# Attention decode over a long cache: the softmax of a four-head chunk taken in two halves, and the last chunks' transfers cut differently

## The chip, the cores and the metric

The kernel runs on one core of a Trainium2 chip. A core has a matrix engine (PE, whose weight loads are listed as PEld), a vector engine (DVE), a scalar engine (ACT), a general engine (POOL), a sequencer that issues transfers (SP), and 16 DMA engines that bring data from HBM to SBUF. Matmuls write to PSUM. The metric is the device time of the whole kernel in microseconds (us). Of the kernel before, four executions were timed: 1372.18, 1374.35, 1375.49 and 1377.13 us, median 1374.92.

## The reference

There are two attention layers with one query per batch row (4 rows, model width 512, 32 heads of 128) over cached keys and values. The first, A, looks at a window of 2048 keys with eight key/value heads; the second, B, at all 8192 keys with 32 heads of its own. The outputs stand side by side.

```python
def _B_ref(x, k_cache, v_cache, wq, wo):        # k_cache, v_cache: [4, 32, 8192, 128] bf16
    q = (x @ wq).reshape(B, Sq, H, Dh).transpose(0, 2, 1, 3)
    scores = jnp.einsum("bhqd,bhkd->bhqk", q, k_cache) * (Dh ** -0.5)
    p = _softmax(scores, axis=-1)
    o = jnp.einsum("bhqk,bhkd->bhqd", p, v_cache)
    return o.transpose(0, 2, 1, 3).reshape(B, Sq, H * Dh) @ wo
```

B's caches are 2 x 268 MB, so nearly all of the 587 MB that the kernel reads is theirs, and each byte is used once.

## The kernel before, in words

The work is cut into 40 chunks. Chunks 0 to 7 are A's (one key/value head each, all batch rows). Chunks 8 to 39 are B's: one batch row and four heads each, with 8.4 MB of keys and 8.4 MB of values. The four heads lie on the partitions, 32 partitions to a head, and each partition holds 64 KB of keys: 256 tiles (`NTB`) of 128 x 128. Tiles go in groups of eight (`TG`), 32 groups to a chunk. `NC` is 40, `NCA` is 8.

One chunk of B (`whole_B`) runs as follows.

1. Keys. For each group, PE transposes eight tiles into a PSUM bank (`emit_T`, bank `tr`), DVE (two of three groups) or ACT (the third) copies them to SBUF (`kt`), and PE multiplies them with the query (`emit_S`, two groups behind, `SLAG`), which leaves the scores in `sc`, one PSUM bank for each half of the keys.
2. Softmax. DVE takes the row maximum of each half (`stats_rowmax`), the first among the scores, and combines the two. PE transposes the maxima (`stats_gmax`), DVE reduces them per head, PE spreads them back over the partitions (`stats_bc`), DVE scales them to `negb`, and ACT takes twelve exps (`exp_B`: three parts of the keys, four heads each) into `pbb`.
3. While this goes on, PE multiplies the rows of B's output weights into another order (`reorder`, four heads; DVE copies each to `wol` with `take_wol`) and runs a few matmuls whose result nobody reads (`keep_busy`).
4. PV. PE multiplies 256 value tiles with the exps, all into one sum in `po` (`emit_pv`). `norm_sum` sums the row sums over the partitions and inverts them, `norm_out` scales `po`. The multiplication with the output weights (`emit_fin`) stands at the second group of the next chunk.

Each engine executes its own list in order, and the lists are written out by the order of the calls in `whole_B`. The wait for an event holds back everything behind it on that engine. The loop over B's chunks is a loop on PE, DVE and ACT; SP and POOL have straight lists.

Transfers are all in SP's list, in the order keys, (for every fourth chunk the output weights `wos`), values (`dma_K`, `dma_V`). Keys land in units 0 to 3 of the buffer `kv`, values in units 4 to 7. The second half of each is then copied by POOL into units 8 and 9 (`KX`), which keys and values share, so a unit is free once its half has been copied. A transfer of keys is issued once the first quarters of the keys before it have been transposed and their second half copied. A transfer of values waits until the first half of the PV before it is done (`("pv", c, 2)`) and the second half of those values has been copied; the copies of values into `KX` wait for the transposes of the keys that lie there. `wos` waits for the fourth `reorder` of the chunk before.

A transfer can be cut into pieces, each with its own semaphore, so that work can begin on a part: `HALVES`, `NEXTK` (four quarters), `NEXTV` (128, 64, 32 and 32 tiles), `LASTK`, `LASTV`. Before the change, keys came in halves in chunks 30 to 34 and in quarters in chunks 35 to 38; values came in halves in chunk 36 and in `NEXTV` in chunks 37 and 38. The last chunk's are cut finest. All other transfers are whole.

The lines of the profile that matter: L475 (transposes) and L477 (all other matmuls), L541 and L543 (copies of transposed keys on ACT and DVE), L612 and L615 (row maximum), L641 (`negb`), L661 (exps), L666 (row sums), L778 (`wol`), L752 (`norm_out`), L372 (POOL's copies), L392 (issue of keys), L355 (of `wos`), L429 (of values).

## Time and profile before

| what | value |
|---|---|
| timed runs, median | 1374.92 us |
| the profiled execution, its own time | 1371.9 us |
| its span, first to last instruction | 1370.1 us |
| PE busy | 1239.1 us (90%) |
| PEld busy | 1114.0 us (81%) |
| DVE busy | 766.9 us (56%) |
| ACT busy | 547.3 us (40%) |
| POOL busy | 469.8 us (34%) |
| HBM read | 587.21 MB, 429 GB/s over the span |
| granted clock of PE, mean | 0.968 |

The span goes from the first to the last instruction on the core; the execution's own time is 1.8 us longer. Busy shares are means over the whole span, and the stages of a chunk use the engines quite differently: PE is nearly always busy among the scores, ACT only copies there, and the exps come in one block behind them. PE's matmuls are pipelined and their ends are modelled, so that a busy PE is not necessarily at its peak. The groups of instructions with the most time:

| line, engine, operation | count | busy us | mean ns |
|---|---|---|---|
| L475 PE, transposes of keys | 8704 | 671.0 | 222 |
| L543 DVE, copies of transposed keys | 736 | 502.1 | 691 |
| L372 POOL, copies of second halves | 248 | 459.9 | 1896 |
| L477 PE, scores of B | 8192 | 399.8 (first form listed) | 192 |
| L541 ACT, copies of transposed keys | 352 | 359.6 | 1024 |
| L477 PE, PV of B | 8192 | 263.2 | 196 |
| L661 ACT, exps of B | 384 | 171.1 | 446 |
| L612 DVE, row maximum of a half | 64 | 43.9 | 686 |
| L666 DVE, row sums | 32 | 39.0 | 1220 |

The durations of single matmuls overlap: the mean of one is longer than the distance from one to the next.

### The profile page before, as it was taken

What the parts mean: (1) busy time and instruction counts of PE and PEld (TensorE: products, weight loads), DVE (VectorE), ACT (ScalarE), POOL (GpSimd) and SP (SyncE); (2) the same over time, 40 slices, a digit from 0 to 9 for tenths busy, and PEclk for the clock granted to TensorE, in tenths of its full rate; (3) what the DMA queues carried; (4) which work ended last, traced back from release to release, by engine and by line L of the source; (5) the groups of instructions that cost most, each with busy time, mean ns of one, the idle gap of its engine ahead of it and who ended that gap; (6) DMA issues with size and microseconds to landing.
All of it is one profiled execution on the core that took longest, in us unless ns stands there. A gap on an engine that the chain in (4) does not pass through costs nothing.

```text
span 1370.1 us, 61779 instructions
## 1 busy us (share of the span) xinstructions
PE 1239.1 (90%) x27640; PEld 1114.0 (81%) x27673; DVE 766.9 (56%) x1335; ACT 547.3 (40%) x777; POOL 469.8 (34%) x277
## 2 busy tenths in 40 slices
PE   4897799988999989888999899998999999999998
PEld 4776688887888878877888788887888888888887
DVE  1775465554555655555556555554565665645555
ACT  1553343443434434433444333433444443433443
POOL 2000244334433443344334433443344334443342
PEclk9998899999999999999999999999999999999999
DMA  9999999999999999999999999999999999999998
GB/s 399 425 427 440 431 427 436 427 438 430 430 436 419 444 438 432 429 430 442 429 429 430 442 429 429 438 435 429 434 430 430 433 433 440 429 422 429 426 426 350
DMA packets 19359, 587.54 MB, mean 429 GB/s; under 512 B 2164, under 2 KB 2184, under 8 KB 4616
## 3 DMA queue, kind: packets, MB, share of 16 engines
q1 hardware_dynamic: 19304, 587.21, 99.6%
q8 instruction: 15, 0.25, 0.1%
q14 instruction: 8, 0.07, 0.0%
q10 hardware_dynamic: 32, 0.01, 0.0%
HBM read 587.21 MB, written 0.01 MB: 429 GB/s over the span
## 4 chain that ended last, share of the span: by engine, by line
DMA 56%; PE 37%; DVE 2%; issue 2%; POOL 2%; ACT 0%; SPq 0%; POOLq 0%; DVEq 0%
DMA kv<-in_B_k_cache_dram 40%; PE tr L475 20%; DMA kv<-in_B_v_cache_dram 11%; PE sc L477 9%; PE po L477 5%; DMA kv<-in_A_k_cache_dram 2%; DMA kv<-in_B_wq_dram 2%; POOL kv L372 2%; PE fin L477 2%; PE ms L477 1%; PE tr L477 1%; DVE rm L615 0%; DVE kt L543 0%; DVE sA L596 0%; DVE wor L778 0%
## 5 line engine op out<-in xcount | busy, mean ns | idle before, releaser
L372 POOL COPY kv<-kv 128x2048 int32<-128x2048 int32 x248 | 459.9, 1896 | 877.3 <-DMA kv<-in_B_k_cache_dram 288.2
L475 PE MATMUL tr<-identb,kv 128*128 128x128 bf16 x8704 | 671.0, 222 | 52.0 <-POOLq L75 44.0
L543 DVE COPY kt<-tr 128x1024 bf16<-128x1024 bf16 x736 | 502.1, 691 | 267.1 <-PE tr L475 264.6
L541 ACT ACTIVATE kt<-tr 128x1024 bf16<-128x1024 bf16 x352 | 359.6, 1024 | 662.6 <-PE tr L475 662.4
L475 PEld LDWEIGHTS tr<-identb,kv 128*128 128x128 bf16 x8704 | 512.6, 99 | 66.0 <-issue 46.7
L477 PE MATMUL sc<-qq,kt 128*128 128x64 bf16 x8192 | 399.8, 192 | 12.5 <-DVE kt L543 9.8
L477 PEld LDWEIGHTS sc<-qq,kt 128*128 128x128 bf16 x8192 | 333.3, 98 | 16.2 <-DVE kt L543 13.1
L477 PEld LDWEIGHTS po<-pbb,kv 128*128 128x128 bf16 x8192 | 260.5, 100 | 22.1 <-issue 10.2
L477 PE MATMUL po<-pbb,kv 128*128 128x64 bf16 x8192 | 263.2, 196 | 10.8 <-POOL kv L372 4.9
L661 ACT ACTIVATE pbb<-sc,negb 32x64 bf16<-32x64 f32 (+1 forms) x384 | 171.1, 446 | 143.7 <-DVE negb L641 138.5
L666 DVE TENSOR_REDUCE rsb<-pbb 128x4 f32<-128x1024 bf16 x32 | 39.0, 1220 | 97.9 <-ACT pbb L661 97.9
L778 DVE CAST wor<-tr 128x512 bf16<-128x512 f32 x128 | 80.3, 684 | 2.9 <-PE tr L477 2.9
L477 PE MATMUL tr<-wos,back 32*128 32x512 bf16 x512 | 69.6, 383 | 3.1
L477 PE MATMUL po<-sel,identb 128*128 128x512 bf16 x224 | 68.5, 401 | 0.0
L477 PEld LDWEIGHTS po<-sel,identb 128*128 128x128 bf16 x256 | 20.1, 99 | 39.5 <-issue 30.7
L612 DVE TENSOR_REDUCE rh<-sc 128x4 f32<-128x512 f32 x64 | 43.9, 686 | 14.3 <-PE sc L477 14.3
L477 PEld LDWEIGHTS tr<-wos,back 32*128 32x128 bf16 x512 | 21.7, 93 | 34.4 <-DVE wor L778 19.2
L752 DVE TENSOR_TENSOR oz<-po,rz 128x16 bf16<-128x16 f32 x32 | 5.6, 175 | 68.9 <-PE po L477 68.9
L730 DVE RECIPROCAL rinv<-ms 128x4 f32<-128x4 f32 (+1 forms) x40 | 7.8, 196 | 49.6 <-PE ms L477 49.6
L475 PE MATMUL ms<-identf,rm 128*4 128x128 f32 x40 | 10.9, 272 | 20.5 <-DVE rm L615 17.9
L477 PE MATMUL sc<-qb,kt 128*128 128x64 bf16 (+3 forms) x512 | 25.4, 194 | 0.8 <-DVE gx L633 0.6
L477 PE MATMUL po<-pba,kv 128*128 128x64 bf16 x512 | 20.5, 199 | 3.7 <-issue 2.4
(65 smaller groups left out, 284.4 us busy)
## 6 DMA issues: line engine op xcount, KB each, us to landing
kv<-in_B_k_cache_dram SPq DMA_DIRECT2D x12, 4096.0 KB, 26.4
kv<-in_B_k_cache_dram SPq DMA_DIRECT2D x17, 2048.0 KB, 30.1
kv<-in_B_v_cache_dram SPq DMA_DIRECT2D x5, 4096.0 KB, 28.9
kv<-in_A_k_cache_dram SPq DMA_DIRECT2D x8, 2048.0 KB, 14.5
kv<-in_A_v_cache_dram SPq DMA_DIRECT2D x8, 2048.0 KB, 16.0
kv<-in_B_v_cache_dram SPq DMA_DIRECT2D x3, 2048.0 KB, 27.3
kv<-in_B_k_cache_dram SPq DMA_DIRECT2D x6, 1024.0 KB, 31.5
kv<-in_B_v_cache_dram SPq DMA_DIRECT2D x5, 1024.0 KB, 31.4
```

The lines of the kernel that those rows point to most:

```text
L372: lambda e, x=x: e.tensor_copy(flat(KX, 2)[:, x].bitcast(I32), flat(units, 2)[:, x].bitcast(I32)),
L475: sch.add("pe", lambda e: e.transpose(o, l, r), waits, key)
L477: sch.add("pe", lambda e: e.matmul(o, l, r, start=start, stop=stop), waits, key)
L541: sch.add("act", lambda e: e.activation(dst, src, ACTF.Copy), waits=waits, key=("ev", s))
L543: sch.add("dve", lambda e: e.tensor_copy(dst, src), waits=waits, key=("ev", s))
L612: sch.add("dve", lambda e: e.tensor_reduce(out=rh[:, half, :], in_=src, axis=AX.X, op=ALU.max), waits=[("S", ch["s"] + (half + 1) * ch["NG ...
L661: sch.add("act", lambda e, src=src, dst=dst, pp=pp, u=u: e.activation(dst, src, ACTF.Exp, bias=negb[pp, 0, u:u + 1], scale=scale), waits=[ ...
L666: sch.add("dve", lambda e: e.tensor_reduce(out=rst[1][:, :], in_=probs_of(c).rearrange("p j u -> p u j"), axis=AX.X, op=ALU.add), waits=[( ...
L730: sch.add("dve", lambda e: e.reciprocal(out=ri, in_=ms[:, L0:L0 + n]), waits=[("L", c)], key=("rinv", c))
L752: sch.add("dve", lambda e: e.tensor_tensor(out=o, in0=i0, in1=i1, op=ALU.mult), waits=waits, key=("oT", c))
L778: sch.add("dve", lambda e: e.tensor_copy(wol[:, u, :], o), waits=[("reord", c) if u == 3 else ("reord", c, u)] + [("fin", prev(c))], key=( ...
```

## The change

Each half of the keys gets a maximum of its own. The first half's maximum, its spreading and its exps are placed among the scores of the second half, at fixed groups (`HEADS_AT`). PV of the first half stands right behind the last score; the second half's maximum and exps are placed between its groups. Between the halves, DVE multiplies the sum in `po` with exp of the difference of the two maxima (`fade_B`, `fade_out_B`), into `fd`, and a matmul with the identity brings it back into PSUM as the start of the second half's sum. The row sums are taken per half and joined in the same way. `keep_busy` is gone. The first three `reorder` stand between the halves, the fourth at group 22 of PV, behind `norm_sum`. The first transposes of the next chunk wait for `wol`.

The pieces change too: keys are cut in the last four chunks (halves in 36 and 37, quarters in 38, the last as before), and values in the last three (halves in 37, `NEXTV` in 38, the last as before).

```diff
-        PIECES_K.update({c: ("d_fk", HALVES) for c in range(NC - 10, NC - 5)})
-        PIECES_K.update({c: ("d_nk", NEXTK) for c in range(NC - 5, NC - 1)})
-        PIECES_V = {NC - 4: ("d_hv", HALVES), NC - 3: ("d_nv", NEXTV), NC - 2: ("d_nv", NEXTV), NC - 1: ("d_lv", LASTV)}
+        PIECES_K.update({NC - 4: ("d_fk", HALVES), NC - 3: ("d_fk", HALVES), NC - 2: ("d_nk", NEXTK)})
+        PIECES_V = {NC - 3: ("d_hv", HALVES), NC - 2: ("d_nv", NEXTV), NC - 1: ("d_lv", LASTV)}
...
+                    if c > NCA and g < NTRB:
+                        waits += [("wol", c - 1, 3 if g == 0 else g)]
...
+        HEADS_AT = {23: (0,), 26: (1,), 29: (2, 3)}
...
-        EXPS = ((0, NTB // 4), (NTB // 4, NTB // 2), (NTB // 2, NTB))
-
-        def exp_B(c):
...
+        def exp_B(c, half, heads):
+            for u in heads:
+                pp = HEADS[u][1]
+                src = sc[pp, half, :].rearrange("p (j u) -> p u j", u=4)[:, u, :]
+                dst = probs_B(half)[pp, :, u]
+                waits = [("negb", c, half), ("c_pb", 1)] + ([("pv", c - 1), ("rs", c - 1)] if c > NCA else []) if u == 0 else []
+                sch.add("act", lambda e, src=src, dst=dst, pp=pp, u=u: e.activation(dst, src, ACTF.Exp, bias=negb[pp, half, u:u + 1], scale=scale),
+                        waits=waits, key=("exp", c, half) if u == 3 else None)
...
+        def fade_B(c):
+            sch.add("dve", lambda e: e.tensor_tensor(out=hs[:, 2, :], in0=negb[:, 1, :], in1=negb[:, 0, :], op=ALU.subtract),
+                    waits=[("negb", c, 1)], key=("gap", c))
+            sch.add("act", lambda e: e.activation(hs[:, 3, :], hs[:, 2, :], ACTF.Exp),
+                    waits=[("gap", c)] + ([("rs", c - 1)] if c > NCA else []), key=("fade", c))
+
+        def part_sums_B(c, half):
+            sch.add("dve", lambda e: e.tensor_reduce(out=hs[:, half, :], in_=probs_B(half).rearrange("p j u -> p u j"), axis=AX.X, op=ALU.add),
+                    waits=[("exp", c, half)], key=("psum", c, half))
+
+        def fade_out_B(c):
+            sch.add("dve", lambda e: e.tensor_tensor(
+                out=fd[:, :].rearrange("p (x u) -> p x u", u=4), in0=po[:, 0:NW].rearrange("p (x u) -> p x u", u=4),
+                in1=bcast(hs[:, 3, :], [[0, NW // 4], [1, 4]]), op=ALU.mult),
+                waits=[("pv", c, 2), ("fade", c)], key=("faded", c))
+
         def sums_B(c):
-            sch.add("dve", lambda e: e.tensor_reduce(out=rst[1][:, :], in_=probs_of(c).rearrange("p j u -> p u j"), axis=AX.X, op=ALU.add),
-                    waits=[("exp", c, 2)] + rs_read[NSM], key=("rs", c))
+            sch.add("dve", lambda e: e.tensor_tensor(out=hs[:, 0, :], in0=hs[:, 0, :], in1=hs[:, 3, :], op=ALU.mult),
+                    waits=[("psum", c, 0), ("fade", c)], key=("fsum", c))
+            sch.add("dve", lambda e: e.tensor_tensor(out=rst[1][:, :], in0=hs[:, 0, :], in1=hs[:, 1, :], op=ALU.add),
+                    waits=[("fsum", c), ("psum", c, 1)] + rs_read[NSM], key=("rs", c))
...
-                for k in (1, 2):
-                    if c >= NCA and j == EXPS[k][0] - NW // 4:
-                        waits = [("exp", c, k)]
+                half = c >= NCA and j == NTB // 2
+                if half:
+                    waits = [("exp", c, 1)]
+                    pe_mm(po[:, base:base + n], identf[:, :], fd[:, :], stop=False, waits=[("faded", c)], key=("fdmm", c))
...
-        def keep_busy(n):
-
-            for _ in range(n):
-                pe_mm(po[:, :], identb[:, :], sel4[:, :, :].rearrange("p r x -> p (r x)"))
...
-                if g == ch["NG"] // 2 + SLAG + 1:
+                if g == 19:
                     stats_rowmax(c, 0)
+                if g == 21:
+                    stats_gmax(c, 0)
+                if g == 23:
+                    stats_bc(c, 0)
+                if g in HEADS_AT:
+                    exp_B(c, 0, HEADS_AT[g])
             for g in range(SLAG):
                 emit_S(ch["s_last"] + 1 - SLAG + g)
             stats_rowmax(c, 1)
-            reorder(c, 0, 0)
-            reorder(c, 1, 1)
-            reorder(c, 2, 2)
-            keep_busy(1)
-            stats_gmax(c)
-            keep_busy(1)
-            stats_bc(c)
-            exp_B(c)
-            for u in range(3):
-                take_wol(c, u, u)
-            keep_busy(3)
-            reorder(c, 3, 0)
-            keep_busy(3)
-            take_wol(c, 3, 0)
-            sums_B(c)
             for g in range(ch["NG"]):
                 emit_pv(c, g)
-                if g == 20:
+                if g == 3:
+                    stats_gmax(c, 1)
+                if g == 6:
+                    stats_bc(c, 1)
+                    fade_B(c)
+                    exp_B(c, 1, range(4))
+                    part_sums_B(c, 0)
+                if g == ch["NG"] // 2 - 1:
+                    for u in range(3):
+                        reorder(c, u, u)
+                    fade_out_B(c)
+                    part_sums_B(c, 1)
+                    sums_B(c)
+                    for u in range(3):
+                        take_wol(c, u, u)
+                if g == 22:
                     norm_sum(c)
+                    reorder(c, 3, 0)
+                    take_wol(c, 3, 0)
             norm_out(c)
```

## The prediction

> **What bounds the kernel now.** I read four views in this order: the page's slices, a table of windows, the timeline of one chunk, and the chain of waits. The slices and the queue table come first:
>
> ```profile
> DMA  9999999999999999999999999999999999999998
> GB/s 399 425 427 440 431 427 436 427 438 430 430 436 419 444 438 432 429 430 442 429 429 430 442 429 429 438 435 429 434 430 430 433 433 440 429 422 429 426 426 350
> q1 hardware_dynamic: 19304, 587.21, 99.6%
> ```
>
> The DMA engines are full in every slice, and one queue carries all of it. The windows, with the B chunks grouped by how their transfers are cut (columns: stretch, length, busy time and count of PE, PEld, DVE, ACT, POOL, then granted clock, DMA share, GB/s):
>
> ```profile
> 193.00:967.00 774.00, 708.24 (x15912) 637.36 (x15930) 432.58 (x712) 308.46 (x437) 296.38 (x160) 0.97 1.00 433
> 967.00:1110.00 143.00, 138.62 (x3143) 125.13 (x3145) 84.68 (x142) 60.30 (x86) 51.90 (x28) 0.98 1.00 433
> 1110.00:1300.00 190.00, 176.69 (x4003) 159.41 (x4006) 109.34 (x180) 77.88 (x110) 74.24 (x40) 0.98 1.00 428
> 1300.00:1362.00 62.00, 58.27 (x1306) 51.96 (x1306) 36.84 (x61) 28.06 (x42) 22.45 (x12) 1.00 1.00 425
> 1365.00:1366.00 1.00, 1.00 (x41) 1.00 (x37) 0.00 (x0) 0.00 (x0) 0.00 (x0) 1.00 0.05 20
> ```
>
> Share 1.00 throughout, so there is almost nothing to fill; what differs is the rate: 433 GB/s with whole transfers, 428 with quarters, 425 with the smallest. The stream ends at about 1364.4 us. The trace's packet records say why the rate differs: a packet of 64 KB takes 2.421 us (median), one of 32 KB 1.216, of 16 KB 0.612, of 8 KB 0.313. Each DMA engine moves eight rows per piece, so keys and values of a chunk cost 16 x 2.421 = 38.74 us. This is the period of the kernel.
>
> Does PE set it too? The chain of waits around one chunk (start, duration; a DMA's start is its issue, so 224.70 + 25.97 is its landing), and the same chunk's timeline after its last score:
>
> ```profile
> 224.70 25.97 DMA kv<-in_B_k_cache_dram
> 250.84 1.06 PE tr L475 x16
> ...
> 261.86 27.51 DMA kv<-in_B_k_cache_dram
> 289.54 1.06 PE tr L475 x16
> ```
>
> ```profile
> 273.44 0.35 PE L477 MATMUL sc<-qq,kt 128*128 128x32 bf16 x8 [0.31 <-DVE kt L543]
> 277.13 5.51 ACT L661 ACTIVATE pbb<-sc,negb 32x64 bf16<-32x64 f32 x12 [4.78 <-DVE negb L641]
> 278.81 0.33 SPq L355 DMA_DIRECT2D wos<-in_B_wo_dram  x1
> 279.37 5.13 PE L477 MATMUL po<-pbb,kv 128*128 128x64 bf16 x168
> 283.37 0.33 SPq L429 DMA_DIRECT2D kv<-in_B_v_cache_dram  x1
> 287.32 0.17 DVE L752 TENSOR_TENSOR oz<-po,rz 128x16 bf16<-128x16 f32 x1 [2.07 <-PE po L477]
> ```
>
> PE: transposes and scores 250.84 to 273.79 (22.95), then softmax and PV to 287.49 (13.7), then 2.05 idle until the keys land. So 36.65 us of work stand against 38.7 of transfer: PE waits for DMA, not the reverse. Keys land at 289.37, the next values were issued at 283.37, 6.0 us earlier. Only at 403.65, in a stretch whose clock was 0.69, was a V issue late: the keys before it landed at 406.8, 3.15 us later, and the packet records show a hole of 0.22 us just there. About 3.3 us of lead are therefore enough. All holes in B after its first chunks sum to 0.4 us.
>
> **The change, part by part.**
>
> *Pieces.* Excess per chunk over whole transfers, by the packet times: halves 16 x 1.216 - 8 x 2.421 = 0.09 us, quarters 32 x 0.612 - 19.37 = 0.22, NEXTV (128, 64, 32, 32) 0.26. Keys: five chunks halves to whole (-0.44), one quarters to whole (-0.22), two quarters to halves (-0.26). Values: one halves to whole (-0.09), one NEXTV to halves (-0.17). Fifteen transfers fewer also spare fifteen completion packets of 9 ns per engine (-0.13). Sum **-1.3 us**, on the stream that sets the end. [...] I take -1.3.
>
> *Softmax in halves.* After the last score PE now goes on. From the rows: first 32 PVs at 2.73/88 = 31 ns: 1.0; row maximum 0.69 + 0.16 with 0.4 of handing over, so the transpose (0.27) ends at about 1.6; 24 PVs 0.74 (2.3), broadcast 0.38 (2.7), 72 PVs 2.2 (4.9), twelve reorder matmuls 1.06 (6.0). Beside this: negb 0.16, gap 0.16, the fade's exp (not in the trace; 128x4, nearest row ACT 32x64 at 0.40, so 0.2 to 0.4; 0.3), four exps of 32x128 at 69.5/128 = 0.54 each: ready at 5.8. The fade of po (128x64 from PSUM, not in the trace; between DVE's 0.175 for 128x16 and 0.69 for 128x512; 0.22 by interpolation) lies under the reorder. Its f32 matmul back into PSUM is like the pair ms<-rsb,onesf, 0.36, bounded by 0.27 and 0.8; 0.4. So the second half starts at 6.4, 56 PVs to 8.1, row-sum matmul 0.36, the fourth reorder 0.36 to 1.03, 72 PVs 2.2: end at **11.5 instead of 13.7**. Eight keep_busy matmuls a chunk (0.40 each) go; they lay in this gap. The first half's maximum, broadcast and exps move among the scores: PE gets a 0.27 and a 0.38, DVE 0.28 + 0.16, ACT four exps in three places; DVE and ACT both have room there (per three groups of 2.04 us, DVE is busy 1.37, ACT 1.02). I take +0.7, ends 0.5 and 1.5. PE's chunk: 36.65 - 2.2 + 0.7 = **35.2 us**, idle 3.5 instead of 2.05. On the path: nothing, as DMA covers it. It does buy lead: V's issue waits for the first half of PV, now at 4.9 instead of 9.6 after the last score, and for the POOL copies, two of 1.85 after the last transpose.
>
> *Queue orders.* In SP's queue wos stands before V and waits for the fourth reorder, which moves from 5.0 after the last score (278.81) to about 9.0. V, behind it, then goes at 9.4, against 9.6 today: no loss in the seven chunks where wos is loaded. POOL keeps its order; its copies of keys wait for the end of PV, which comes earlier. The new waits of the first three transposes for wol (DVE, three copies of 0.69 behind the sums, then the fourth) end at about 10.8, before PV's 11.5. If that cover went, transposes and everything behind them on PE would start later, inside 3.5 us of idle time.
>
> *Clock.* [...] The trace has the case:
>
> ```profile
> 480.00:490.00 10.00, 5.89 (x107) 4.99 (x104) 1.73 (x4) 0.93 (x1) 4.34 (x3) 0.83 1.00 433
> 490.00:500.00 10.00, 10.00 (x242) 10.00 (x238) 6.86 (x10) 4.69 (x6) 3.07 (x2) 1.00 0.97 419
> ```
>
> After some 4 us of idle time the clock was 0.83 for one window, 1.7 us lost, while the DMA rate held. [...] by the row nothing, since 1.7 < 3.5. I take nothing.
>
> *Holes.* With 4 us more lead (except where wos goes first) the late V issue goes: **-0.3**, ends 0 and -0.4. Next late is only DMA itself.
>
> *Tail.* The last piece of V landed at 1366.3 by the landing records, and PV ended at 1366.83: PE and DMA finish together, and landing, PV, fin, copy and output follow for 3.8 us, unchanged. PE must again be ahead at the end. With pieces from four chunks before the end it can gain at most its slack of 3.5 plus what the pieces release; I get the last chunk's transposes some 1 us later than today relative to its keys, and 2.2 us less behind the last score. I take **0**, ends -0.1 and +1.5.
>
> Sum against the profiled run: span 1370.1 - 1.3 - 0.3 = 1368.5; the 1.8 us around the span stay: **1370.3 us**. The profiled run (1371.9) lies 3.0 under the median of the four timed runs (1374.92). I read these 3 us as more such late V issues in executions with a worse clock: in this one the lead was thin (3.15 to 6 us) and the clock falls to 0.69 in single stretches. With the longer lead they should go, so 1370.3 should be near the new median. A change of 0.3% (4.1 us) is about what a measurement of this kernel tells from none: faster is below 1370.8, slower above 1379.0.
>
> **Rivals.**
>
> *The spread stays (0.20).* The 3 us are not holes but come with the launch or the memory. For it: the only trace has 0.4 us of holes. Against it: the thin lead. Then the median falls by the pieces and holes of the profiled run alone: 1374.9 - 1.6 = 1373.3.
>
> *PE is late at the end (0.12).* Nine chunks of cut keys become four; if the transposes of the last chunk come 2 to 3 us later, the 11.5 us behind the last score end after the landing by about 2: 1372.3.
>
> *Slower: wos holds V back (0.08).* Place: SP's queue in the seven chunks that load wos. The fourth reorder stands behind the second exps, the fade, the sums and a wol copy. V goes at 9.4 after the last score and may be 6.0 - 3.3 = 2.7 us later before DMA runs dry. Beyond that each us costs 7. If the reorder came 4.2 us later than I have it (second exps delayed, a cold clock): 7 x 1.5 = 10.5, so 1380.8. For it: the wait is new in that place; against it: every step before it is measured or small.
>
> **Numbers.** The forecast has 0.60, its own range 1369.0 to 1371.8, about 0.50 of it below 1370.8. Faster 0.52 (with a little of the second rival), same 0.40, slower 0.08. The range 1369.0 to 1374.0 takes in the first two rivals and leaves out the third and the outer ends.
>
> **What would show it.** Right: rate 433 GB/s up to about 1245 us, a stream some 1.3 us shorter, PE idle about 3.5 us a chunk before each key landing, V issues 9 us or more ahead of the keys' landing (6 with wos), the second half of PV starting about 6.4 us after the last score. Wrong: holes in DMA in wos chunks, a PV that ends well after the last landing, transposes waiting for wol, or new timed runs that still spread over 5 us.

## The result, and the profile after

The changed kernel's median is 1371.92 us (42 executions, 1370.80 to 1375.15); the kernel before, run beside it, has 1373.85 us (63 executions, 1371.49 to 1379.32). The ratio is 0.9985, 95% interval 0.998 to 0.999. So it is faster by 0.15%, a difference that many executions resolve, but inside the 0.3% that the forecast counted as no change. The time lies 1.6 us above the forecast's point, just outside its own range (1369.0 to 1371.8) and inside the wider one that takes in two rivals; "faster", which had the larger chance, did not come.

The executions also lie closer together: their standard deviation went from 1.85 to 0.99 us. The profiled execution took 1370.98 us with a span of 1369.3 (before: 1371.9 and 1370.1). The gain of 1.93 us in the median therefore has two parts, and the end of the stream splits the first again. The last line sets one execution against the median, so it only says where that one lay among the others:

```
                                            before     after    difference
last piece of V lands (landing records)     1366.3    1364.1       -2.2
from there to the end of the span              3.8       5.1       +1.3
time of the profiled execution              1371.9   1370.98       -0.9
median minus profiled execution              +1.95     +0.94       -1.0
```

The slices and the queue of the changed kernel:

```profile
DMA  9999999999999999999999999999999999999998
GB/s 400 426 426 439 433 429 435 433 433 431 429 435 433 434 429 438 442 421 433 442 435 431 427 440 435 429 435 437 431 433 429 440 431 431 429 438 421 427 426 340
...
q1 hardware_dynamic: 17144, 587.21, 99.5%
```

The same bytes in 2160 packets fewer, and DMA is still the limit in every slice. The stretches of B, by how their transfers are now cut (columns as before: busy time and count of PE, PEld, DVE, ACT, POOL, then granted clock, DMA share, GB/s):

```profile
193.00:1187.00 994.00, 897.72 (x20452) 832.69 (x20449) 572.78 (x1099) 375.51 (x485) 378.49 (x204) 0.96 1.00 433
1187.00:1300.00 113.00, 108.48 (x2476) 100.90 (x2477) 73.39 (x132) 45.37 (x58) 44.50 (x24) 0.97 0.99 426
1300.00:1362.00 62.00, 60.48 (x1450) 57.26 (x1447) 41.43 (x78) 28.53 (x37) 22.45 (x12) 1.00 1.00 424
1364.00:1365.00 1.00, 1.00 (x40) 1.00 (x37) 0.45 (x1) 0.00 (x0) 0.00 (x0) 1.00 0.00 0
```

The rate of 433 GB/s now holds up to 1187 us instead of 1110. In the last row DMA has nothing left to bring (share 0.00) while PE works without a pause: the end is no longer PE and DMA together, but PE alone. The last chunk's timeline shows where (start, duration, engine, line, operation; the last score ends at 1355.09):

```profile
1354.74 0.35 PE L478 MATMUL sc<-qq,kt 128*128 128x32 bf16 x8 [0.30 <-DVE kt L546]
1354.96 1.09 PE L478 MATMUL po<-pbb,kv 128*128 128x64 bf16 x32
...
1357.29 2.27 PE L478 MATMUL po<-pbb,kv 128*128 128x64 bf16 x72
...
1360.48 0.43 PE L478 MATMUL po<-fd,identf 128*128 128x64 f32 x2
1360.76 1.80 PE L478 MATMUL po<-pbb,kv 128*128 128x64 bf16 x56
...
1362.68 1.03 PE L478 MATMUL tr<-wos,back 32*128 32x512 bf16 x4
1363.65 2.27 PE L478 MATMUL po<-pbb,kv 128*128 128x64 bf16 x72
```

PV starts right behind the last score, its second half 5.7 us after it, and it ends at 1365.92, that is 10.8 us after the last score and 1.8 after the last landing at 1364.1.

**What the two traces showed when laid side by side.** In the middle of B (chunks 9 to 31) the time from the last score to the end of PV was 12.6 us in eight chunks of the kernel before, 12.8 to 13.5 in eleven, and 15 to 16.9 in four. One small operation varies with it: the `tensor_tensor` at L615 that combines the maxima of the two halves, 128x4 elements, both operands in SBUF. By form, before and after (columns: count, busy us, mean ns, then idle time ahead of it):

```profile
L615 DVE TENSOR_TENSOR rm<-rh 128x4 f32<-128x4 f32 x32 | 21.1, 658 | 1.1
```

```profile
L619 DVE TENSOR_TENSOR rm<-rm 128x4 f32<-128x4 f32 x32 | 13.4, 418 | 1.1
L677 DVE TENSOR_TENSOR hs<-negb 128x4 f32<-128x4 f32 x32 | 8.8, 275 | 1.1
L694 DVE TENSOR_TENSOR hs<-hs 128x4 f32<-128x4 f32 x32 | 7.1, 221 | 0.0
```

A mean of 658 ns for 512 numbers hides two kinds. In eight of the 32 chunks POOL copies nothing meanwhile, and L615 takes 0.16 us. In the other 24 it starts while POOL copies second halves, 1.9 us a copy. In six of these the running copy ends within 0.13 us, and L615 still takes 0.16; in the other 18 it takes 0.32 to 1.86, and every time it ends within 0.02 us of the end of that copy (worked out from the trace's records). Two lines of the same trace stand on either side of it. L612, which reads PSUM (128x512), takes 0.68 to 0.69 us in the 29 cases in which POOL is copying when it starts, as in the 35 others. L735, a `tensor_tensor` of 128x16 with both operands in SBUF, takes 0.18 us in 27 chunks and 0.48 to 1.83 in the five in which POOL is copying. So the operation that read PSUM was free of this wait here, and those with two SBUF operands were not; what makes them wait, the trace does not show. The forecast had taken L615 at its 0.16 us. Even in the chunk whose timeline it shows, from 273.44 on, it took 1.26:

```profile
274.55 1.26 DVE L615 TENSOR_TENSOR rm<-rh 128x4 f32<-128x4 f32 x1
```

The chunk in which the forecast had found its one late V issue (403.65) is such a chunk, too; timeline of the kernel before:

```profile
389.46 5.57 POOL L372 COPY kv<-kv 128x2048 int32<-128x2048 int32 x3
...
391.21 0.69 DVE L612 TENSOR_REDUCE rh<-sc 128x4 f32<-128x512 f32 x1 [0.45 <-PE sc L477]
391.94 1.27 DVE L615 TENSOR_TENSOR rm<-rh 128x4 f32<-128x4 f32 x1
...
393.26 0.27 PE L475 MATMUL ms<-identf,rm 128*4 128x128 f32 x1 [1.09 <-DVE rm L615]
```

L615 ends at 393.21, as the second of the three copies behind each other does (389.46 + 2 x 1.86 = 393.18), and PE, which needs `rm`, waits 1.09 us. What the clock did meanwhile stands in windows laid on the steps of its records (3.41 us):

```profile
390.48:393.89 3.41, 1.87 (x24) 0.84 (x23) 2.52 (x4) 0.00 (x0) 3.41 (x3) 1.00 0.89 384
393.89:397.30 3.41, 3.40 (x9) 1.19 (x9) 1.96 (x4) 2.49 (x7) 1.14 (x1) 0.50 1.15 500
397.30:400.70 3.40, 3.40 (x38) 2.25 (x38) 1.16 (x2) 2.82 (x6) 0.00 (x0) 0.50 0.85 366
```

After a stretch in which PE was busy 1.87 of 3.41 us, the granted clock is 0.50 in the next two (6.83 us by the clock's records). This chunk (the row of 16.43) beside five others of the kernel before (worked out from the trace's records; all times us):

```
L615     half clock     last score to end of PV
0.16        0              12.60
0.61        0              12.88
1.26        0              13.54
1.28       3.41            15.06
1.27       6.83            16.43
1.55       6.83            16.90
```

Without the clock the delay is passed on nearly one for one (12.6 plus what L615 has over 0.16); with it, another 1.3 to 2.9 us come on top. A long L615 does not always bring the half clock: of the nine chunks from 9 on in which it took 1.26 us or more, four lost the clock and five kept it. This gave the theory for the experiments: **the gain, and the spread that went, come from this wait leaving PE's path.** In the changed kernel the same kind of operation (L619) lies beside PV and delays it by 0.57 us at most in the middle of B. The rivals were the forecast's own terms: that the block of softmax as such held V's issue back, or that the pieces bring the gain.

### The profile page after: what moved, and what is told of

Its sections match the earlier page's. It is cut to its first block, busy times and chain, and to the rows that moved or that the text cites. A ratio compares the mean times of both kernels' runs of the same rounds, so it can differ in the third digit from the quotient of the medians.

```text
span 1369.3 us, 62176 instructions
## 1 busy us (share of the span) xinstructions
PE 1222.3 (89%) x27576; PEld 1130.3 (83%) x27577; DVE 792.0 (58%) x1559; ACT 521.6 (38%) x681; POOL 470.3 (34%) x277
## 4 chain that ended last, share of the span: by engine, by line
DMA 56%; PE 40%; DVE 2%; issue 1%; ACT 0%; SPq 0%; POOLq 0%; DVEq 0%; ACTq 0%
DMA kv<-in_B_k_cache_dram 53%; PE tr L476 23%; PE sc L478 10%; PE po L478 3%; PE fin L478 2%; DMA kv<-in_B_wq_dram 2%; DMA kv<-in_A_k_cache_dram 1%; PE ms L478 1%; PE tr L478 1%; DVE sA L600 1%; PE ms L476 0%; DVE kt L546 0%; ACT pba L713 0%; DVE rm L612 0%; DVE rm L619 0%
## 5 line engine op out<-in xcount | busy, mean ns | idle before, releaser
L476 PE MATMUL tr<-identb,kv 128*128 128x128 bf16 x8704 | 687.7, 225 | 91.6 <-POOLq L75 87.0
L544 ACT ACTIVATE kt<-tr 128x1024 bf16<-128x1024 bf16 x352 | 359.6, 1024 | 714.3 <-PE tr L476 714.0
L476 PEld LDWEIGHTS tr<-identb,kv 128*128 128x128 bf16 x8704 | 528.7, 101 | 109.4 <-issue 102.4
L478 PEld LDWEIGHTS sc<-qq,kt 128*128 128x128 bf16 x8192 | 336.0, 99 | 16.9 <-DVE kt L546 13.1
L669 ACT ACTIVATE pbb<-sc,negb 32x128 bf16<-32x128 f32 x256 | 138.6, 542 | 6.3 <-DVE negb L647 1.5
L616 DVE TENSOR_REDUCE rm<-sc 128x4 f32<-128x512 f32 x64 | 43.9, 686 | 14.3 <-PE sc L478 14.3
L683 DVE TENSOR_REDUCE hs<-pbb 128x4 f32<-128x512 bf16 x64 | 43.5, 680 | 13.0 <-ACT pbb L669 13.0
L647 DVE TENSOR_SCALAR negb<-ms 128x4 f32<-128x4 f32 x64 | 10.4, 163 | 43.0 <-PE ms L478 43.0
L688 DVE TENSOR_TENSOR fd<-po,hs 128x64 f32<-128x64 f32 x32 | 7.2, 225 | 41.4 <-PE po L478 41.4
L476 PE MATMUL ms<-identf,rm 128*4 128x128 f32 x72 | 19.8, 275 | 10.8 <-DVE rm L619 7.2
L478 PE MATMUL fin<-wor,oz 128*4 128x256 bf16 x264 | 28.8, 360 | 0.4 <-DVE oz L784 0.4
L632 DVE TENSOR_REDUCE gm<-ms 4x4 f32<-4x128 f32 x72 | 19.8, 275 | 15.3 <-PE ms L476 15.3
```

Of the source, the lines that this page charges most:

```text
L476: sch.add("pe", lambda e: e.transpose(o, l, r), waits, key)
L478: sch.add("pe", lambda e: e.matmul(o, l, r, start=start, stop=stop), waits, key)
L544: sch.add("act", lambda e: e.activation(dst, src, ACTF.Copy), waits=waits, key=("ev", s))
L616: sch.add("dve", lambda e: e.tensor_reduce(out=rm[:, half, :], in_=src, axis=AX.X, op=ALU.max), waits=[("S", ch["s"] + (half + 1) * ch["NG ...
L632: sch.add("dve", lambda e: e.tensor_reduce(out=gm[0:C, m, 0:U], in_=src, axis=AX.X, op=ALU.max), waits=[("trm", c, half)], key=("gmax", c, ...
L647: sch.add("dve", lambda e: e.tensor_scalar(out=negb[:, m, 0:C], in0=ms[:, col:col + C], scalar1=-scale, scalar2=None, op0=ALU.mult), waits ...
```

## The experiments

The executions of the kernel before that were run beside these have medians from 1373.38 to 1375.47 us; each ratio is to those on the same chip. The ratios are given as recorded; they are not the quotients of the two medians, and they, rather than medians from different chips, are what two versions can be compared by.

**1. The new pieces in the kernel before.**

```diff
...
+        PIECES_K.update({NC - 4: ("d_fk", HALVES), NC - 3: ("d_fk", HALVES), NC - 2: ("d_nk", NEXTK)})
+        PIECES_V = {NC - 3: ("d_hv", HALVES), NC - 2: ("d_nv", NEXTV), NC - 1: ("d_lv", LASTV)}
```

> The kernel before with the new pieces alone, softmax as before. My theory: the pieces shorten the DMA stream (last landing about 1364 to 1365 us instead of 1366.3), but a PE with 2 us of idle time in a chunk of 36.7 us cannot get ahead within four chunks: the last chunk's transposes start about 1335 instead of 1330.5 and PV ends some 7 us after the last landing, so the span is about 1375 and the time about 2 to 5 us above before. Rival (the pieces carry the gain by themselves): 1 to 2 us below before.

Median 1377.49 (20 executions, 1372.24 to 1386.02, standard deviation 4.27), ratio 1.0028 (1.0013 to 1.0044): slower. Alone the pieces cost 3.3 us and double the spread. The loss is of the size that was expected. The profiled execution was the fastest of all (1372.24) and doesn't show it: PV ends 1.8 us after the last landing there, not 7. Hence number 2.

**2. The same two kernels, profiled once more.** No edit: the kernel before and the kernel of number 1, in the hope of a longer execution.

> The kernel before, unchanged: a second execution to look into. 49 further runs of it lie between 1371.4 and 1378.5 us, and their time falls with the granted clock (correlation -0.7). My theory of the forecast: what a slow execution has over 1371.9 lies in holes of the DMA stream behind late V issues in the middle of B (each hole where the lead over the keys' landing is under 3.3 us). Rival: the stream is whole, and the excess lies at the end, where PV ends after the last landing because PE could not get ahead. A fast execution (under 1373) tells neither.

1373.19 us. The last landing came at 1367.6 instead of 1366.3, and 3.8 us behind it the end as before: the whole excess is in the stream.

> The kernel before with the new pieces alone, once more: its twenty runs lie between 1372.2 and 1386.0, and only the fastest was profiled. My theory: in a usual execution (1375 and more) the DMA stream is about as long as in the fast one (last landing 1365 to 1366 us), and PE is late at the end: the last chunk's transposes start at 1334 us or later instead of 1331.65, and PV ends more than 4 us after the last landing. Rival: holes in the stream in the middle of B, with the end as in the fast one.

1380.72 us, 8.5 over number 1's profile. The last landing came at 1372.9 instead of 1365.3, so 7.6 of it are in the stream and only 0.9 in the tail: the expectation of a late end missed, and that number 1 came out at the expected size was luck. Seven chunks spread over B have 16.4 to 17.2 us behind the last score, and just these seven issue their values late. Its L614 (the same operation, a line higher) has a mean of 830 ns, against 603 in number 1's profile:

```profile
L614 DVE TENSOR_TENSOR rm<-rh 128x4 f32<-128x4 f32 x32 | 26.6, 830 | 1.1
```

How this reaches the stream can be read from the issues and landings of the profiled executions (worked out from the records; numbers 3 to 5 follow below; the 26 whole transfers of values issued between 195 and 1200 us). A landing of values follows that of the keys by 19.4 us, or 20.6 with `wos` between them, when nothing is late; "late" is what it has over that:

```
                              V issued under 3.3 us        values late by      last piece
                              ahead of the keys' landing   in sum              of V lands
kernel before                 2 times                      0.4                 1366.3
kernel before, once more      4                            1.6                 1367.6
number 1                      2                            0.5                 1365.3
number 1, once more           7                            7.1                 1372.9
changed kernel                0 (least lead 4.5)           0                   1364.1
number 3                      0 (3.3)                      0                   1365.4
number 4                      0 (4.0)                      2.3                 1368.6
number 5                      0 (4.0)                      0.7                 1365.1
```

The late issues follow the wait, and most of the lost stream lies behind them. But a lead of 3.3 us is no limit: of the seven in number 1's second profile four cost 1.1 to 2.4 us and three nothing, while in number 4 leads of 4.1 to 6.3 us cost 0.2 to 0.8 each, five times, without L615.

**3. The softmax in halves with the old pieces.**

```diff
...
+        PIECES_K.update({c: ("d_fk", HALVES) for c in range(NC - 10, NC - 5)})
+        PIECES_K.update({c: ("d_nk", NEXTK) for c in range(NC - 5, NC - 1)})
+        PIECES_V = {NC - 4: ("d_hv", HALVES), NC - 3: ("d_nv", NEXTV), NC - 2: ("d_nv", NEXTV), NC - 1: ("d_lv", LASTV)}
```

> The changed kernel with the pieces of before. My theory: last landing back at about 1366 us (fifteen more transfers, smaller packets), but the tail from the last landing to the end back at 3.8 us instead of 5.2, so the span is 1369.5 to 1370 and the median about 0.5 us above the changed kernel's, still about 1 us below before, with a spread as narrow as the changed kernel's. Rival (the halved softmax does not matter under DMA): median and spread as before.

1371.74 (19 executions, standard deviation 0.92), ratio 0.9986 (0.9978 to 0.9994). That is the whole gain of the change (0.9985): what the pieces add lies inside the intervals. The narrow spread is here too. The profiled execution (1373.02, 1.3 above its kernel's median) has its last landing at 1365.4, 1.3 later than the changed kernel's, just the forecast's sum for the pieces. Its tail is 5.9 us, not the 3.8 that was expected: chunks 31 to 36 have 13.7 to 17.2 us behind the last score, and the clock falls in the last.

**4. The row maximum as one reduction, in the kernel before.** This takes away L615 and leaves the rest of the block as it is, but for the maximum itself: one reduction over 1024 columns after the last score instead of one over 512 among the scores, one behind them and the joining.

```diff
-            src = sc[:, half, :].rearrange("p (j u) -> p u j", u=4)
-            sch.add("dve", lambda e: e.tensor_reduce(out=rh[:, half, :], in_=src, axis=AX.X, op=ALU.max),
...
-                sch.add("dve", lambda e: e.tensor_tensor(out=rm[:, m, :], in0=rh[:, 0, :], in1=rh[:, 1, :], op=ALU.max),
...
+            src = sc[:, :, :].rearrange("p h (j u) -> p u (h j)", u=4)
+            sch.add("dve", lambda e: e.tensor_reduce(out=rm[:, m, :], in_=src, axis=AX.X, op=ALU.max),
+                    waits=[("S", ch["s_last"])], key=("rowmax", c))
```

> The kernel before, with the row maximum taken in one reduction over both halves behind the last score (128x1024, about 1.35 us) instead of two of 0.69 and a combining tensor_tensor of two SBUF operands. In the traces of before that tensor_tensor takes 0.16 us, but 0.3 to 1.9 while POOL copies, and every softmax longer than 15 us in the middle of B stands behind one of 1.07 us or more, with the clock at half for 3.4 or 6.8 us. My theory (this wait on POOL, and the clock that falls because of it, make the late V issues and the spread of before): softmax and PV take 13.1 us in nearly every chunk of the middle, none over 15, and the median falls to about 1372 with a standard deviation near 1 us instead of 1.9. Rival (the clock falls by itself): as many stretches over 15 us, median and spread as before.

1371.43 (20 executions, standard deviation 1.13), beside 1373.38 (54 executions, 1.87): ratio 0.9981 (0.9974 to 0.9988). By form:

```profile
L612 DVE TENSOR_REDUCE rm<-sc 128x4 f32<-128x1024 f32 x32 | 39.2, 1224 | 14.3 <-PE sc L477 14.3
```

1224 ns on PE's path in every chunk, where 686 + 160 would do if POOL were quiet; and it is faster. From the last score to the end of PV it is 12.77 us in each chunk of the middle (12.74 to 12.79), none over 15 there (six chunks near the end, where PE waits for values, have 14.2 to 16.8). So in the middle the spread of this time was L615's, and leaving out one operation of 512 numbers gives -1.95 us, as much as the whole change (-1.93), with the softmax still in one block. The rival theory, that the block as such was the cost, falls. That the changed kernel gains through the same wait follows from the equal sizes and from its even chunks; no run has the halves with the wait still on PE's path. Nor is the wait all: the profiled execution (1374.28) is among the slowest of its kernel and lands its last piece at 1368.6, with no L615 in it.

**5. The same with the new pieces.**

```diff
...
+        PIECES_K.update({NC - 4: ("d_fk", HALVES), NC - 3: ("d_fk", HALVES), NC - 2: ("d_nk", NEXTK)})
+        PIECES_V = {NC - 3: ("d_hv", HALVES), NC - 2: ("d_nv", NEXTV), NC - 1: ("d_lv", LASTV)}
```

> The kernel one_max (softmax as before, but no combining tensor_tensor) with the new pieces. With the combining operation these pieces gave 1377.5 us and a standard deviation of 4.3. My theory (PE got too late for them by waiting on POOL and by the clock that fell behind it, not because the softmax stands in one block): softmax and PV take 12.8 us in every chunk of the middle, the last chunk's transposes start at about 1331.7, PV ends some 2 us behind the last landing (1365), span about 1370.5, median about 1372, standard deviation near 1. Rival (the block of softmax itself makes PE too slow for four chunks of pieces): 1376 us and more.

1371.46 (13 executions, 1370.62 to 1372.60, standard deviation 0.67), ratio 0.9975 (0.9967 to 0.9984); 12.77 us behind the last score in all chunks but the first and one near the end (13.2). Number 1 has the same pieces with L615, and 1377.49: the pieces harm only where that wait makes PE late. With the wait gone they don't harm; whether they help by up to 0.8 us (ratio 0.9975 with them, 0.9981 without) lies inside the intervals.

**6. The fourth reorder behind PV, in the changed kernel.** It tests the third rival and the lead that DMA needs.

```diff
                 if g == 22:
                     norm_sum(c)
+                if g == 31:
                     reorder(c, 3, 0)
                     take_wol(c, 3, 0)
```

> The changed kernel with the fourth reorder and its wol copy behind the last group of PV instead of group 22, 2.3 us later. In the seven chunks that load wos, V is issued behind wos, now 2.2 us ahead of the keys' landing instead of 4.5. My theory (3.3 us of lead are needed): holes of about 1.1 us in the DMA stream in each of these chunks, 7 to 8 us in all, so 1379. Rival (lead does not matter above zero): no holes and the changed kernel's time.

1379.61 (8 executions), ratio 1.0032 (1.0019 to 1.0045): slower, as expected. The profiled execution (1383.22, the slowest of the eight) has its last landing 10.5 us later than the changed kernel's. SP's queue at the first chunk that loads `wos`, in the changed kernel and then in this one:

```profile
284.53 0.33 SPq L357 DMA_DIRECT2D wos<-in_B_wo_dram  x1
284.90 0.42 SPq L431 DMA_DIRECT2D kv<-in_B_v_cache_dram  x1
```

```profile
286.64 0.33 SPq L357 DMA_DIRECT2D wos<-in_B_wo_dram  x1
287.02 0.42 SPq L431 DMA_DIRECT2D kv<-in_B_v_cache_dram  x1
```

The keys before them land at 289.4 in both. A lead of 4.5 us left DMA at share 0.98 in the window 285 to 288; with 2.4 that window shows the hole:

```profile
285.00:288.00 3.00, 1.61 (x27) 0.82 (x22) 0.94 (x3) 0.00 (x0) 0.00 (x0) 1.00 0.52 195
```

The next keys land at 331.2 instead of 329.3. In the seven chunks with `wos` the lead is 1.5 to 2.8 us and the values land 0 to 2.2 us late, 7.1 in all. The mechanism of the third rival is real, and the changed kernel is at most 2.1 us away from it.

**7. A warm clock, in the changed kernel.** Eight matmuls whose result nobody reads at the head of each chunk, to fill the idle time that `keep_busy` no longer fills.

```diff
+            if c > NCA:
+                for i in range(8):
+                    pe_mm(tr[:, 2, :].bitcast(F32), identb[:, :], sel4[:, :, :].rearrange("p r x -> p (r x)"),
+                          waits=[("wol", c - 1, 2)] if i == 0 else [])
```

> The changed kernel with eight matmuls of 512 columns, whose result nobody reads, at the head of each chunk of B but the first, where PE waits for keys. The clock then stays up: transposes and scores should take 23.5 us a chunk instead of 25.0. My theory: the 1.5 us are hidden, as DMA sets the period; the time stays within 0.7 us of the changed kernel (1371.9). In the last four chunks, which don't wait, the eight matmuls cost 1.7 us each on PE, so the end may come 1 to 4 us later. Rival (the cold clock is paid on the path[...]): 20 us and more faster.

1384.87 (4 executions), ratio 1.0085 (1.0063 to 1.0107); at most 0.7 us had been expected. Most of the loss is no price of the clock: at the loop's first pass PE stands still for 6.81 us that no wait explains, holes of some 5.6 us in DMA follow at 189 to 217 us, and from chunk 12 to chunk 34 each chunk starts 7.3 to 7.8 us later than in the changed kernel.

```profile
176.38 3.10 PE L478 MATMUL tr<-sel,identb 128*128 128x512 bf16 x7 [6.81 <-issue]
```

In the middle, transposes and scores take 23.48 us in more than half of the chunks (the changed kernel: about 25.0 in most, where the granted clock is 0.50 for 2.8 to 6.0 us near the head, and 23.48 where it is 1.00), but the keys land 38.7 us apart as without. So a cold start costs 1.5 us a chunk and DMA covers it.

**8. Finer pieces in the changed kernel.** First only the values of the third chunk from the end, then keys and values of one chunk more each.

```diff
-        PIECES_V = {NC - 3: ("d_hv", HALVES), NC - 2: ("d_nv", NEXTV), NC - 1: ("d_lv", LASTV)}
+        PIECES_V = {NC - 3: ("d_nv", NEXTV), NC - 2: ("d_nv", NEXTV), NC - 1: ("d_lv", LASTV)}
```

> The changed kernel, with the values of the third chunk from the end cut 128, 64, 32, 32 instead of in halves. My theory: PE is late at the end because this chunk's PV waits for POOL's copies of a half that lands whole (14.6 us behind the last score instead of 10.9); with finer pieces it ends about 2.5 us sooner, the last chunk starts that much sooner, PV ends at the last landing (about 1364.6), the tail is 3.8 to 4.2 us, the span about 1368.2, the time 1 us below the changed kernel. Rival (the last chunk is bound by its own keys' landing): no change in the tail of 5.2 us.

1370.79 (11 executions), ratio 0.9978 (0.9965 to 0.999): 1.1 under the changed kernel's median, though the two did not run beside each other. The profiled execution (1372.65) doesn't show the mechanism: near the end, where PE waits for values and POOL's copies fall beside the second maximum, two chunks have 13.9 us behind the last score, with

```profile
1282.90 1.72 DVE L619 TENSOR_TENSOR rm<-rm 128x4 f32<-128x4 f32 x1
```

and 3.41 us of half clock. This L619, too, ends within 0.02 us of the POOL copy that ran when it began: the wait that was L615's is still there.

```diff
+        PIECES_K.update({NC - 5: ("d_fk", HALVES), NC - 4: ("d_fk", HALVES), NC - 3: ("d_fk", HALVES), NC - 2: ("d_nk", NEXTK)})
+        PIECES_V = {NC - 4: ("d_hv", HALVES), NC - 3: ("d_nv", NEXTV), NC - 2: ("d_nv", NEXTV), NC - 1: ("d_lv", LASTV)}
```

> The changed kernel with cut transfers from one chunk earlier: keys in halves from the fifth chunk from the end, values in halves in the fourth and 128, 64, 32, 32 in the third and second. My theory: the stream grows by 0.35 us, but PE starts the last chunk 2 to 4 us sooner and ends with the last landing: span about 1368.3, median 1370.3 to 1370.6, 1.3 to 1.6 us below the changed kernel. Rival (PE cannot use earlier keys, since values and POOL's copies hold it): the changed kernel's time plus 0.3.

1371.29 (16 executions), ratio 0.9981 (0.9972 to 0.999), above the expected 1370.3 to 1370.6; the last chunk's transposes start no sooner (1331.55 against 1331.62 in the changed kernel). Cutting more bought nothing that shows.

**9. The row sums joined out of PSUM**, on top of the finer values of number 8, so that L694 and L696 no longer have two SBUF operands. In the changed kernel's trace these take 0.15 and 0.16 us, but 0.55 to 1.54 (L694, three times) and 1.80 (L696, once) while POOL copies.

```diff
-            sch.add("dve", lambda e: e.tensor_tensor(out=hs[:, 0, :], in0=hs[:, 0, :], in1=hs[:, 3, :], op=ALU.mult),
-                    waits=[("psum", c, 0), ("fade", c)], key=("fsum", c))
-            sch.add("dve", lambda e: e.tensor_tensor(out=rst[1][:, :], in0=hs[:, 0, :], in1=hs[:, 1, :], op=ALU.add),
...
+                pe_mm(ms[:, L0:L0 + 8], onesf[:, :], hs[:, 0:2, :].rearrange("p a u -> p (a u)"),
+                      waits=[("psum", c, 0), ("psum", c, 1), "c_onesf"] + ms_read, key=("L", c))
+                sch.add("dve", lambda e: e.tensor_tensor(out=rs, in0=ms[:, L0:L0 + 4], in1=hs[:, 3, :], op=ALU.mult),
...
+                sch.add("dve", lambda e: e.tensor_tensor(out=rs, in0=ms[:, L0 + 4:L0 + 8], in1=rs, op=ALU.add),
```

> The changed kernel with the finer values of v_finer, and with the row sums joined behind the matmul over the partitions, so that no DVE operation there has two SBUF operands: PE multiplies both halves' sums in one matmul of 8 columns, DVE joins them from PSUM. My theory: in the last four chunks PE no longer waits for those two operations (1.0 to 1.8 us each during POOL's copies) and the clock stays up behind them, so softmax and PV take about 11 to 12 us there instead of 13 to 14, PV ends with the last landing (tail 3.8 us instead of 5.2), span 1367.9 to 1368.5, median about 1370.2. Rival (values and copies hold PE there anyway): as v_finer, 1370.8.

1372.00 (20 executions), ratio 0.9987 (0.9979 to 0.9994). The median missed. The executions lie in two clusters, nine from 1370.19 to 1370.47 and eleven from 1371.93 to 1373.41; the profiled one is of the first (1370.46), with a tail of 4.4 us. No trace shows what the second has more, so this run decides nothing.

**10. All four reorders between the halves as well**, the fourth into the first bank of the scores, on top of number 9.

```diff
-            o = tr[:, bank, :].bitcast(F32)
+            o = tr[:, bank, :].bitcast(F32) if u < 3 else sc[:, 0, :]
...
-                    for u in range(3):
+                    for u in range(4):
                         reorder(c, u, u)
...
                 if g == 22:
                     norm_sum(c)
-                    reorder(c, 3, 0)
-                    take_wol(c, 3, 0)
...
```

> As port, and all four reorders between the halves, the fourth into the scores' first bank, free by then. In chunks that load wos, V is then issued some 6.5 us after the last score instead of 9, so its lead over the keys' landing grows from 4.5 to about 7 us. My theory: the holes of up to 0.5 us in these chunks go, and median and spread are a little under those of port: 1369.9 to 1370.3. Rival (the lead of 4.5 us is enough, and what is left of the spread comes from elsewhere): as port.

1370.67 (18 executions, 1369.59 to 1371.77, standard deviation 0.63), ratio 0.9979 (0.9972 to 0.9986); that is below number 9 and above the expected 1369.9 to 1370.3. Behind `wos` the lead is 6.5 to 7.7 us, as expected. From the last score to the end of PV it is 9.83 us in nearly all chunks of the middle, and the end is DMA's again:

```profile
1364.41 0.41 PE L478 MATMUL po<-pbb,kv 128*128 128x64 bf16 x8 [0.22 <-POOLq L75]
1364.85 0.17 DVE L787 TENSOR_TENSOR oz<-po,rz 128x16 bf16<-128x16 f32 x1 [1.26 <-PE po L478]
...
1366.33 0.35 SPq L847 DMA_DIRECT2D out_dram<-outsb  x1
```

PE's last eight matmuls wait for the last piece (landed at 1364.3), and the tail is 3.8 us, against 5.1. This version has the lowest median of all, with the narrowest spread of these runs. It is faster than before; to the changed kernel, which did not run beside it, the distance is 1.25 us of medians, and the intervals of the two ratios overlap a little.

## Why the prediction was right and wrong

**The bound: right.** DMA sets the period (keys land 38.7 us apart where no `wos` lies between), PE waits for it; whatever shortened or lengthened PE inside a chunk (1.7 to 2.7 us less behind the last score, the clock's 1.5) moved the end only through the stream or the tail.

**Pieces, -1.3: right for the stream, not seen in the time.** In the profiled executions the last landing is sooner with the new pieces than with the old in all three pairs: 1.0 us in the kernel before, 1.3 with the softmax in halves, 3.5 with one reduction. Each is a single execution; with the late values of number 2's table taken off they are 1.1, 1.3 and 1.9. Yet both pairs of ratios say no change that is clear of noise: 0.9986 and 0.9985 with the softmax in halves, 0.9981 and 0.9975 with one reduction. That the later end of PE gives it back would fit two pairs of tails (3.8 to 5.2, 4.0 to 4.6), but not the third (5.9 to 5.1); where it goes stays open.

**Holes, -0.3: the size by luck.** The forecast names 403.65 as the only late issue and read its hole as lost time. This issue moved no landing: its values land at 426.1 in both kernels. Another one that it missed, in the half-clocked chunk whose L615 took 1.27 us (898.93), was later still:

```profile
910.83 0.33 SPq L429 DMA_DIRECT2D kv<-in_B_v_cache_dram  x1
```

The keys land at 913.76, 2.93 us after it, and the values at 934.8, 0.4 us later than in the changed kernel. So the term has its size from a place that the forecast did not name, and its "About 3.3 us of lead are therefore enough" rested on one hole; number 2's table shows no such limit.

**The softmax: steps right, sizes close.** The second half of PV starts 5.7 us after the last score (forecast 6.4), PV ends at 10.8 to 11.4 (11.5), transposes and scores take 0.53 us longer where the clock is up (0.7), PE mostly idles 2.8 to 3.8 us (3.5). V's lead is 7.8 to 11.7 us without `wos`, mostly over 9 (V issued at 319.37, keys landed at 329.3), as written; behind `wos` it is 4.5 to 5.5, not 6. But the 13.7 that the 11.5 stood against was a chunk with 1.1 us of L615's wait in it (the row of 274.55), and counts `norm_out` too: PV's end came at 12.6 where L615 was quiet, so about half of the forecast 2.2 was this wait, which the forecast had at nothing.

**The clock at nothing: right.** It is at 0.50 near the head of 21 of the 31 chunks from 9 on now (9 before) and costs mostly 1.5 us in each, below the idle time; number 7 shows that taking it away moves no landing in the middle.

**The tail at 0: the size failed.** The term was 0 with ends of -0.1 and +1.5; it measured +1.3. The last chunk's transposes come 1.1 us later than before, as written (1331.62 against 1330.52), but the last landing comes 2.2 sooner and PV's end only 0.9. The second rival is what happened at the end, at 1371.92 near its 1372.3: PE is the late one, 1.8 us after the last landing, though its transposes were not the 2 to 3 us later that it names.

**The spread: right place, wrong origin, wrong size.** "I read these 3 us as more such late V issues in executions with a worse clock": the second profile of the kernel before (number 2) has its excess of 1.3 there, 1.0 of it behind one V issue. But four executions overstated it; over 63 the median lies 1.95 above the profiled one, of which 1.0 went. And the step missed where late V issues came from. The forecast took the clock as given and L615 as its 0.16 us, "0.69 + 0.16 with 0.4 of handing over"; it did not look at the spread behind a group's mean of 658 ns. The experiments put the origin at that operation waiting for POOL: without it, and with nothing else of the change, the gain and the even chunks are there (number 4). The clock is a weaker witness. In the kernel before, an execution is longer the lower its mean granted clock (correlation -0.70 over 49 executions, but -0.31 over 21 others on another chip); in the changed kernel there is no such link (+0.09 over 44), yet in number 10, where the spread is narrowest, there is one (-0.75 over 18).

The sum of the miss: stream 0.6 better, tail 1.3 worse, and 0.9 between the profiled execution and the median that should have been nil, together 1.6 us.

What stays open: what the remaining 0.9 us of spread are, with the two clusters of number 9 among them and the stream lost in number 4's profile; and what makes the clock fall. L615 alone does not decide it: five of nine long ones left the clock up, and in the kernel before it was at half for 6.83 us from 1206.26 on, in a chunk whose L615 took 0.17 and whose PV waited for values.

## What to carry to other kernels

Where a small operation stands on the path of every chunk, look at the spread of its durations, not at the group's mean: the 128x4 operation here that took 0.16 us in one chunk and 1.3 in another was waiting for another engine. Where a vector operation gates the matrix engine while the general engine copies, take its input from PSUM, as number 4 does: reading PSUM, L612 took its 0.68 to 0.69 us and L641 (128x4) its 0.16 under copies as without them. That was worth as much here as a new order of the softmax. And when the transfers set the period, judge a change by landings and tail separately, over many executions: time won on the stream can be lost again at the end.

## What was not expected of the hardware

- A DVE `tensor_tensor` of 128x4 with both operands in SBUF took 0.16 us alone and up to 1.86 while POOL copied 128x2048 (1.9 us each); 18 of 18 long ones ended within 0.02 us of the copy's end (L615, kernel before).
- The granted clock fell to one half, for 3.41 or 6.83 us, behind windows of 3.41 us in which PE was still busy for 1.87 to 2.21: such half-filled windows came before five of the 13 drops from chunk 9 on. Others with 1.5 to 2.2 us of work did not bring one; all eight with less than 1.4 did, and none with more than 2.3 (kernel before, windows laid on the grid of the clock's records).
- How far ahead the next transfer must be issued has no sharp limit here: 2.4 us ahead of the landing before it cost 0 to 1.9 us (number 6), 4.1 to 6.3 cost up to 0.8 in number 4's profile, and 4.5 and more cost nothing in the changed kernel.
- Matmuls put at the head of the loop on PE cost 6.81 us once, at the first pass, with no wait in the trace (number 7, at 176.38).
